# Mask products exchanged between VectorE and GpSimd, copies of keys and queries moved, and global outputs normalized for two quads at a time in the steady batches of an attention and feed-forward kernel

## The chip, the cores and the metric

The kernel runs on one core of a Trainium2 chip. The metric is the device time of one execution in microseconds (us). Before the change the median of three runs is 285.36 us (285.32 to 285.50).

## The reference

Eight batches (B = 8) of eight heads (H = 8) with 512 local and 32 global positions each, and a head dimension of 64. A local query sees all 32 global keys and the local keys at most 32 positions away; a global query sees everything. The outputs of all heads of one position form a row of 512, and each of the 4352 rows goes through a feed-forward layer with a sigmoid-approximated GELU.

```python
k_all = np.concatenate([k_g, k_l], axis=2)
v_all = np.concatenate([v_g, v_l], axis=2)
out_g = np.matmul(sm(scale * np.matmul(q_g, k_all.transpose(0, 1, 3, 2))), v_all)
mask = np.abs(pos[:, None] - pos[None, :]) <= 32
s_ll = np.where(mask, scale * np.matmul(q_l, k_l.transpose(0, 1, 3, 2)), -1000000000.0)
s_lg = scale * np.matmul(q_l, k_g.transpose(0, 1, 3, 2))
out_l = np.matmul(sm(np.concatenate([s_lg, s_ll], axis=-1)), v_all)
x = np.concatenate([out_g, out_l], axis=2).transpose(0, 2, 1, 3).reshape(4352, 512)
h = x @ w_in                                   # 4352 x 2048
out = (h * (1.0 / (1.0 + np.exp(-1.702 * h)))) @ w_out
```

## The kernel before

**Tiling.** The four heads of one half of a batch are a quad: 16 quads, two to a batch, called `a` (first) and `c` (second). A quad's keys and queries lie four heads by 32 partitions, as pairs of bf16 numbers in f32 words, so that one 32x32 transpose of f32 words (`Tk`, L512, and `Tq`, L316) puts the head dimension on partitions. Because of the window, the local scores of a quad are computed in two rounds of parts (`S(0)`, `S(1)`, L560): each is a set of 32-row matmuls into four PSUM banks, then an exponential on ScalarE (`X`, L571, two instructions), then a product in place with a 0/1 mask of bf16 (`M`, L576).

For these parts a quad needs some copies: `kcopy` (L504) and `qcopy` (L507) put keys and queries that lie apart side by side, and `ext` (L538 to L545, four parts) puts the global queries and keys beside the local ones. `transpose_g` (L244) transposes global queries and keys.

**Outputs of attention.** `U(0)` sums the masked exponentials with a matrix of ones, `U(1)` and `U(2)` multiply them with the two halves of the values (L586, 24 matmuls each), and `Gm` (L597, 20 matmuls) gives the numerators and denominators of the global queries in one bank `og`. `UG` is all four. `R` (L462 to L466) transposes the sums, takes reciprocals and transposes back; `XL(0)` and `XL(1)` (L471) write the normalized local outputs `xL`. `G` (L476 to L479) takes the reciprocal of the denominator in `og`, multiplies, and transposes into `xG`, which the feed-forward layer reads as a ninth block at the very end.

**Feed-forward.** `h_step` (L617) makes 128 of the 2048 hidden features for one batch's 512 local rows, `h_act` (L622) applies the GELU. One pair of features blocks is made in seven products instead of eight, as a Strassen scheme (`HPair`, L699), from sums of `xL` that `x_sums` (L673, L674) makes on VectorE; its additions are `z`, `zm`, `sub`, `add` (L707 to L716), its GELUs `inner` and `outer`. The second matrix is done for all of a batch in the same scheme, in two halves of rows: `Pair` (products L800; `m3` and `evict` on ScalarE, L113; `z`, `zm`, `sub`, `add` on VectorE, L812 to L825; `store` by SP's queue). Its left sums `g_sums` (L770, L773) are on VectorE.

**Order.** The order is written out by hand (no scheduler): each engine runs its instructions in the order of the program, and waits at semaphores. From i = 3 on a batch alternates between two stages. `h_some(i)` is the first matrix of batch i (its first TensorE line is `hp L617 x8`); between its steps come the transposes and copies for quad `c` of batch i+1 and quad `a2` of batch i+2. `phase_o(i)`, called for i = 2 to 6, is the second matrix of batch i (`p0`, `p1`) interleaved with the rest of the attention of batch b = i+1: quad `a` was scored before, `c` is scored in it, and so is quad `a2` of batch i+2. Its `loads_after(i + 1)` issues on GpSimd's queue the nine transfers of values (L98, L100) and the two of queries and keys (L81, L82) of later batches, with a cast from f32 to bf16.

**PSUM.** The scores and the pair of `HPair` share four banks. The other four (pool `psP`, tag `p`) are handed out in turn. In `phase_o` the order is: `a`'s three `ov` and `og`, then px and py of `p0`, `c`'s three `ov` and `og`, then px and py of `p1`, then the `hp` of the next stage. So px of `p0` takes the bank of `a`'s U(0) once `R` has transposed it, `c.U(2)` takes the bank of px of `p0` once `evict` has read it, and the third `hp` of `h_some` to use this pool (feature block 4) takes px of `p1`.

Of the kernel before, what the change touches and what calls it, by code (L numbers as in the profile page):

```python
# [12 lines left out]
F32 = mybir.dt.float32  # L13
BF16 = mybir.dt.bfloat16
# [6 lines left out]
def kernel(  # L21
# [12 lines left out]
    nc = tc.nc  # L34

    B, H, Sl, D = q_l.shape
# [23 lines left out]
    att = ctx.enter_context(tc.tile_pool(name="att", bufs=2))  # L60
# [14 lines left out]
    def load(b, us=(0, 1), kq=True):  # L75
        if b not in loaded:
            loaded[b] = (ld.tile([128, 2, 16 * D], BF16, name="rk"),
                         ld.tile([128, 2, 16 * D], BF16, name="rq"))
        if kq:
            s = slice(us[0], us[-1] + 1)  # L80
            nc.gpsimd.dma_start(out=loaded[b][1][:, s], in_=qf[b][:, s])  # L81
            nc.gpsimd.dma_start(out=loaded[b][0][:, s], in_=kf[b][:, s])  # L82
# [8 lines left out]
    def load_v(b, hs=slice(0, 8)):  # L91
        if b == 2:
            nc.gpsimd.memset(v_view(b, 5)[:, :, :, :, D:], 1.0)
        vt = v_view(b, 5).rearrange("p u j c d -> p (u j) c d")
        vs, vg = (x[b].rearrange("h s d -> s h d") for x in (v_l, v_g))
        for c in range(5):
            n = 128 if c == 2 else 96
            nc.gpsimd.dma_start(out=vt[0:n, hs, c, :D], in_=vs[FIRST[c] : FIRST[c] + n, hs])  # L98
            if c != 2 and b != 1:
                nc.gpsimd.dma_start(out=vt[96:128, :, c, :D], in_=vg)  # L100
# [11 lines left out]
    def on_act(out_, in_):  # L112
        nc.scalar.activation(out_, in_, AF.Copy)  # L113
# [11 lines left out]
    def load_g(lo, hi, names="kq"):  # L125
        for name, dst, src in (("k", rkg, kgf), ("q", rqg, qgf)):
            if name in names:
                nc.gpsimd.dma_start(out=dst[:, lo:hi, :], in_=src[:, lo:hi, :])
# [111 lines left out]
    def transpose_g(lo, hi, names="qk"):  # L240
        for name, dst, s in (("q", qgT, rqg), ("k", kgT, rkg)):
            if name not in names:
                continue
            nc.vector.transpose(dst[:, lo:hi, :32], s[:, lo:hi].bitcast(F32))  # L244
# [31 lines left out]
    xG_by_row = xG.rearrange("p k (a s f) -> p k a s f", a=2, f=4)  # L276
# [7 lines left out]
    def spair():  # L284
        return [psS.tile([128, 2, 512], F32, name="s4", tag="s%d" % i) for i in range(2)]

    def bank(pair, j):
        return pair[j // 2][:, j % 2, :]
# [211 lines left out]
    class Wide(Quad):  # L500
# [100 lines left out]
        def UG(self):  # L601
            for unit in range(3):
                self.U(unit)
            self.Gm()

    gTs, ops = {}, {}
    HT = TB // 2
    HM = d_model // 2
# [23 lines left out]
    def gelu_table():  # L632
        gelu(spot[:, 0:1], spot[:, 1:2])

    def exp_table():
        nc.scalar.activation(spot[:, 0:1], spot[:, 1:2], AF.Exp)
# [27 lines left out]
    def x_sums(i):  # L664
        t = xL[i]
        x11, x12, x21, x22 = (t[:, 2 * k : 2 * k + 2, h * HT : h * HT + HT] for k in range(2) for h in range(2))
        r1 = att.tile([128, 16, 32], F32, name="sT", bufs=1).rearrange("p a b -> p (a b)").bitcast(BF16)
        r2 = att.tile([128, 512], F32, name="rs", bufs=1).bitcast(BF16)
        xs["d"] = [r.rearrange("p (k t) -> p k t", k=2) for r in (
            r1[:, : 2 * HT], r1[:, 2 * HT :], moe.tile([128, 2 * HT], BF16, name="xs"))]  # L670
        xs["s"] = r2.rearrange("p (k t) -> p k t", k=NKC)
        for o, x, y, op in zip(xs["d"], (x11, x12, x21), (x22, x22, x11), (ALU.add, ALU.subtract, ALU.subtract)):
            nc.vector.tensor_tensor(o, x, y, op)  # L673
        nc.vector.tensor_tensor(xs["s"], t[:, :, :HT], t[:, :, HT:], ALU.add)  # L674
        xs["r"] = (x11, x22)
# [173 lines left out]
    a, c = Quad(0), Quad(1)  # L849
# [93 lines left out]
    a, c = nq[1]  # L943
# [71 lines left out]
    a, c = nq[2]  # L1015
# [22 lines left out]
    def loads_after(i):  # L1038
        if i + 2 < B:
            load_v(i + 2)  # L1040
        if i == 1:
            load_g(8, NQ)
        if i + 3 < B:
            load(i + 3)

    def quads_of(n):
        if n < B and n not in nq:
            nq[n] = (Wide(2 * n), Wide(2 * n + 1))
        return nq.get(n, (None, None))
# [44 lines left out]
    def phase_o(i):  # L1094
        b = i + 1
        a, c = nq[b]
        a2, c2 = quads_of(b + 1)
        p0, p1 = Pair(i, 0), Pair(i, 1)
        exp_table()
        a.UG()  # L1100
        c.S(0)
        a.R()
        g_sums(i, 7, 8, (0,))
        a.XL(0)
        g_sums(i, 7, 8, (1, 2))
        a.XL(1)
        g_sums(i, 7, 8, (3,))
        p0.mm(3, 4, 1)
        c.X(0)
        p0.m3()  # L1110
        p0.z()
        a.G()
        c.M(0)
        c.S(1)
        c.X(1)
        p0.mm(6)
        p0.zm()
        c.M(1)
        p0.mm(5, 2)
        p0.sub()  # L1120
        p0.evict()
        p0.mm(7)
        p0.add()
        p0.store()
        if a2:
            c.UG()
            c.R()
            a2.S(0)
            a2.X(0)
            a2.M(0, nc.gpsimd)  # L1130
            loads_after(i + 1)
        else:
            pt = spair()
            c.U(0, bank(pt, 0))
            c.U(1, bank(pt, 2))
            c.U(2, bank(pt, 3))
            c.Gm(bank(pt, 1))
            c.R()
        c.XL(0)
        if a2:  # L1140
            c.XL(1)
            c.G()
        p1.mm(3, 4)
        p1.m3()
        p1.z()
        if not a2:
            c.XL(1)
            c.G()
        p1.mm(1, 6)
        p1.zm()  # L1150
        x_sums(i + 1)
        if a2:
            a2.S(1)
            a2.X(1)
        p1.mm(5, 2)
        p1.sub()
        p1.evict()
        gelu_table()
        p1.mm(7)
        p1.add()  # L1160
        if a2:
            a2.M(1)
        p1.store()

    def h_some(i):
        c = nq[i + 1][1] if i + 1 < B else None
        a2 = quads_of(i + 2)[0] if i + 2 < B else None
        pool = nc.gpsimd.tensor_copy
        gTs[i] = moe.tile([128, FC, TB], BF16, name="gT")
        hps = [pbank("hp"), pbank("hp")]  # L1170
        for fc in range(2):
            h_mm(i, fc, hps[fc], range(NKC))
        p = HPair(i, 1)
        p.mm(3, 4)
        p.m3()
        for fc in range(2):
            h_act(i, fc, hps[fc])
        if c:
            c.Tk(False)
            c.kcopy(pool)  # L1180
        p.z()
        p.mm(1, 6)
        p.zm()
        if c:
            c.Tq(False)
            c.qcopy(pool)
            c.ext((3,), pool)
        if a2:
            a2.Tk(False)
            a2.kcopy(pool)  # L1190
        h_step(i, 4)
        if c:
            c.ext((0,), on_act)
        h_step(i, 5)
        p.mm(5, 2)
        p.sub()
        p.inner()
        p.mm(7)
        p.add()
        h_step(i, 6)  # L1200
        p.outer()
        if a2:
            a2.Tq(False)
            transpose_g(2 * i + 4, 2 * i + 6)
            a2.qcopy(pool)
            a2.ext(copy=pool)
        if c:
            g_sums(i, 0, 2)
        h_step(i, 7)
        if c:  # L1210
            c.ext((1,), on_act)
            g_sums(i, 2, 4)
            for fc in range(8, 12):
                h_step(i, fc)
                if fc == 9:
                    c.ext((2,), on_act)
            g_sums(i, 4, 6)
            h_step(i, 12)
            h_step(i, 13)
            g_sums(i, 6, 7)  # L1220
            h_step(i, 14)
            h_step(i, 15)
            return
        p = HPair(i, 4)
        p.mm(3, 4)
        p.m3()
        g_sums(i, 0, 2, (0, 1))
        p.z()
        p.mm(1, 6)
        p.zm()  # L1230
        g_sums(i, 0, 2, (2,))
        h_step(i, 10)
        h_step(i, 11)
        p.mm(5, 2)
        p.sub()
        p.inner()
        p.mm(7)
        p.add()
        g_sums(i, 0, 2, (3,))
        h_step(i, 12)  # L1240
        p.outer()
        for k in range(3):
            for lo in (2, 4):
                g_sums(i, lo, lo + 2, (k,))
        h_step(i, 13)
        h_step(i, 14)
        h_step(i, 15)
        g_sums(i, 6, 8, (0, 1, 2))
        g_sums(i, 2, 4, (3,))
        g_sums(i, 4, 6, (3,))  # L1250
        g_sums(i, 6, 8, (3,))

    for i in range(1, B):
        if i > 2:
            h_some(i)
        elif i > 1:
            for fc in range(FC):
# [3 lines left out]
                if i + 1 < B:  # L1261
                    c = nq[i + 1][1]
# [6 lines left out]
                    if fc == 9 and i + 2 < B:  # L1269
                        a2 = quads_of(i + 2)[0]  # L1270
# [19 lines left out]
    for st in range(FC):  # L1290
        h_step(B, st)
        if st < len(todo):
            tt, k = todo[st]
            if k == 3:
                p = Pair(B - 1, tt, pair_banks(tt))
# [19 lines left out]
    p = Pair(B, 0, (x0, x1, y0, y1))  # L1315
# [53 lines left out]
```

## Time and profile before

| what | value |
|---|---|
| median of three runs | 285.36 us |
| the profiled execution | 285.70 us |
| its span, first to last instruction | 284.0 us |
| granted TensorE clock | 1.00 |
| busy: TensorE, VectorE, ScalarE, GpSimd | 277.0, 228.9, 182.1, 107.1 us |
| phase_o(3), 131.0 to 148.6 us: VectorE, ScalarE, GpSimd busy (of 17.65) | 16.4, 10.8, 4.7 us |
| h_some(4), 148.7 to 163.7 us: VectorE, ScalarE, GpSimd busy (of 15.00) | 14.7, 12.1, 9.4 us |

The profile names PE (TensorE), DVE (VectorE), ACT (ScalarE), POOL (GpSimd) and SP (SyncE, which issues the stores). A line of the chain of waits or of a timeline gives start and duration in us, engine, operation, what it writes and reads, and how many of them; in brackets stands the idle time of the engine before it and what ended it. A `kT<-kT` on POOL is a kcopy, a `qc<-q` a qcopy, an `e<-e,mask` an M, an `sT<-xL` the first two x_sums, `gs<-gT` are g_sums.

### The profile page before, as it was taken

How to read it: one execution, taken by the hardware profiler on the slowest of the kernel's cores; microseconds unless marked ns; L12 is line 12 of the kernel's file. 1: busy time of each engine (PE TensorE's matmuls, PEld its weight loads, DVE VectorE, ACT ScalarE, POOL GpSimd, SP SyncE). 2: the span in 40 equal slices, each digit the busy share in tenths (PEclk: the TensorE clock that was granted, in tenths of full speed). 3: DMA queues.
4: the chain of work that ended last, by engine and by line, in shares of the span. 5: the costliest groups of instructions: out<-in, count | busy, mean ns of one | idle time of the engine just before them, and what ended most of it. 6: DMA issues, size and time to landing. Idle time of an engine off the chain costs nothing.

```text
span 284.0 us, 9001 instructions
## 1 busy us (share of the span) xinstructions
PE 277.0 (98%) x3763; PEld 182.3 (64%) x3763; DVE 228.9 (81%) x518; ACT 182.1 (64%) x299; POOL 107.1 (38%) x172
## 2 busy tenths in 40 slices
PE   7899999999999999999999999999999999999994
PEld 6454445544554488746885588647875589558884
DVE  7584458986689899999989998999988898586452
ACT  4858757577778784688457873788459761873331
POOL 8993550765946001990079302960041000000001
PEclk9999999999999999999999999999999999999999
DMA  7999995899999801795039802980022003200223
GB/s 208 159 195 210 203 162 77 148 217 144 170 165 183 151 2 48 78 177 91 14 69 163 150 5 68 84 97 3 21 58 74 2 3 76 74 3 0 58 54 112
DMA packets 59352, 28.24 MB, mean 99 GB/s; under 512 B 47472, under 2 KB 49776, under 8 KB 59312
## 3 DMA queue, kind: packets, MB, share of 16 engines
q0 software_dynamic: 51760, 17.83, 56.2%
q1 hardware_dynamic: 7120, 9.18, 11.7%
q8 instruction: 29, 0.48, 0.7%
q10 hardware_dynamic: 432, 0.66, 0.7%
q14 instruction: 11, 0.09, 0.1%
HBM read 36.31 MB, written 8.91 MB: 159 GB/s over the span
## 4 chain that ended last, share of the span: by engine, by line
PE 86%; DVE 7%; DMA 2%; issue 1%; POOL 1%; ACT 1%; DVEq 0%; POOLq 0%; ACTq 0%
PE hp L617 31%; PE px L800 12%; PE op L731 10%; PE py L800 9%; PE x L800 6%; PE s L560 5%; PE ov L586 5%; PE s L699 3%; PE s L617 3%; DMA rq<-in_q_l_dram 2%; DVE gs L773 2%; DVE gs L770 1%; DVE xL L471 1%; DVE kT L512 1%; PE og L597 1%
## 5 line engine op out<-in xcount | busy, mean ns | idle before, releaser
L617 PE MATMUL hp<-xL,w_in_sb 128*128 128x512 bf16 x432 | 97.0, 379 | 0.2 <-DVE xL L471 0.2
L617 PEld LDWEIGHTS <-w_in_sb 128*128 128x128 bf16 x528 | 51.4, 98 | 51.8 <-issue 0.4
L622 ACT ACTIVATE gT<-hp 128x512 bf16<-128x512 f32 x108 | 62.7, 600 | 17.1 <-PE hp L617 16.6
L571 ACT ACTIVATE e<-s 128x1016 bf16<-128x1016 f32 (+1 forms) x56 | 53.3, 1003 | 25.7 <-PE s L560 25.7
L800 PEld LDWEIGHTS <-gs 128*128 128x128 bf16 x480 | 46.2, 98 | 6.6
L576 POOL TENSOR_TENSOR e<-e,mask 128x1760 bf16<-128x1760 bf16 x4 | 13.3, 3320 | 70.0 <-ACT e L571 70.0
L98 POOL DMA_DIRECT2D v<-in_v_l_dram x40 | 31.1, 780 | 13.6 <-PE og L597 3.8
L773 DVE TENSOR_TENSOR gs<-gT 128x512 bf16<-128x512 bf16 (+1 forms) x87 | 31.6, 398 | 3.3 <-ACT gT L622 3.3
L800 PE MATMUL py<-wsum,gs 128*128 128x256 bf16 x240 | 30.3, 273 | 0.0
L731 PE MATMUL op<-w_out_sb,gT 128*128 128x512 bf16 x128 | 29.5, 380 | 0.0
L576 DVE TENSOR_TENSOR e<-e,mask 128x1712 bf16<-128x1712 bf16 (+1 forms) x24 | 25.2, 1049 | 3.5 <-ACT e L571 3.5
L512 DVE STREAM_TRANSPOSE kT<-rk 128x512 f32<-128x512 f32 x14 | 14.5, 1037 | 12.6 <-DMA rk<-in_k_l_dram 12.6
L833 POOL DMA_DIRECT2D out_dram<-ob x2 | 1.2, 596 | 60.5 <-ACT ob L113 60.3
L731 PEld LDWEIGHTS <-gT 128*128 128x128 bf16 x128 | 11.8, 98 | 14.0
L800 PEld LDWEIGHTS <-gT 128*128 128x128 bf16 x192 | 18.0, 98 | 3.0
L800 PE MATMUL px<-w_out_sb,gT 128*128 128x256 bf16 x160 | 19.2, 273 | 0.1
L800 PE MATMUL px<-w_out_sb,gs 128*128 128x256 bf16 x160 | 19.1, 273 | 0.0
L471 DVE TENSOR_TENSOR xL<-ov,rs 128x512 bf16<-128x512 f32 x27 | 17.9, 686 | 1.0 <-PE ov L438 0.3
L113 ACT ACTIVATE ob<-px 128x512 f32<-128x512 f32 x10 | 6.0, 599 | 19.3 <-DVE zz L822 19.3
L770 DVE TENSOR_TENSOR gs<-gT 128x1024 bf16<-128x1024 bf16 (+1 forms) x29 | 17.2, 598 | 0.0
L560 PEld LDWEIGHTS <-kT 32*128 32x128 bf16 x672 | 12.5, 93 | 6.8 <-issue 5.7
L100 POOL DMA_DIRECT2D v<-in_v_g_dram x24 | 14.0, 585 | 2.2 <-DMA rq<-in_q_l_dram 1.7
(176 smaller groups left out, 429.3 us busy)
## 6 DMA issues: line engine op xcount, KB each, us to landing
out_dram<-ob SPq DMA_DIRECT2D x128, 64.0 KB, 2.7
rq<-in_q_l_dram POOLq DMA_DIRECT2D x5, 512.0 KB, 8.2
rk<-in_k_l_dram POOLq DMA_DIRECT2D x5, 512.0 KB, 10.0
v<-in_v_l_dram POOLq DMA_DIRECT2D x24, 96.0 KB, 4.8
w_in_sb<-in_moe_w_in_dram POOLq DMA_DIRECT2D x8, 256.0 KB, 6.9
w_out_sb<-in_moe_w_out_dram POOLq DMA_DIRECT2D x4, 512.0 KB, 10.1
rk<-in_k_l_dram POOLq DMA_DIRECT2D x5, 256.0 KB, 7.8
rq<-in_q_l_dram POOLq DMA_DIRECT2D x5, 256.0 KB, 7.2
```

The lines of the kernel that those rows point to most:

```text
L98: nc.gpsimd.dma_start(out=vt[0:n, hs, c, :D], in_=vs[FIRST[c] : FIRST[c] + n, hs])
L471: nc.vector.tensor_mul(self.x[:, 2 * self.u + h, :], self.st[1 + h], self.st["rs"])
L512: nc.vector.transpose(flat[:, 0:Sl].rearrange("p (r t) -> p t r", t=16), loaded[self.b][0][:, self.u].bitcast(F32))
L560: nc.tensor.matmul(bank(self.ps, j)[:, at : at + n], lhsT=self.k[p, KEYS[c] : KEYS[c] + 128, e], rhs=qs[p, :, :, e], start=(e == 0), stop= ...
L571: nc.scalar.activation(self.E[rnd][:, 2 * i : 2 * i + 2, :n], self.ps[i][:, :, :n], AF.Exp, scale=scale)
L576: eng.tensor_mul(e, e, mask[:, rnd : rnd + 1, :n].to_broadcast([128, 4, n]))
L617: nc.tensor.matmul(hp[:, : width(i)], lhsT=w_in_c[:, fc // 4, kc, fc % 4 // 2, :, fc % 2], rhs=(xL[i] if i < B else xG)[:, kc, :], start=( ...
L622: nc.scalar.activation(out_, in_, AF.Gelu_apprx_sigmoid)
L731: nc.tensor.matmul(op, lhsT=gTs[i][:, fc, tci * 128 : tci * 128 + 128], rhs=w_out_sb[:, fc, :], start=(first and fc == 4 * f4), stop=(fc = ...
L770: nc.vector.tensor_tensor(sums[i][2][:, g, :n], t[:, g, 0, :n], t[:, g, 1, :n], ALU.add)
L773: nc.vector.tensor_tensor(sums[i][k][:, g, : n // 2], x[:, g], y[:, g], op)
L800: nc.tensor.matmul(out_, lhsT=lv[:, g, tt * 128 : tt * 128 + 128], rhs=rv[:, g, :], start=(g == 0 and k in ((1, 3, 4, 6) if self.apart els ...
```

## The change

In `phase_o`, for all of its calls:
- `a.G()` and `c.G()` are gone. `keep_og` copies each quad's `og` from PSUM to an SBUF tile `ogs` on ScalarE (66 columns), and `GG` normalizes both quads at once on VectorE: one reciprocal, one product, two transposes.
- `a2.M(0)` moves from GpSimd to VectorE, and from behind `a2.X(0)` to behind `p1.z()`; `a2.M(1)` moves from VectorE to GpSimd.
- `loads_after` moves out of `phase_o` into the following `h_some`, behind the copies of `c` on GpSimd.

In `h_some(i)`, i from 3: the transposes of `c` and `a2` come earlier in VectorE's order, ahead of the additions of `HPair`. The kcopy, qcopy and ext of `a2`, which GpSimd did there, move to ScalarE in the following `phase_o` (i = 3 to 5): kcopy and qcopy ahead of the exponential `c.X(1)`, ext behind it.

TensorE's instructions and their order are the same. (`i > 2` and `a2` together are i = 3, 4, 5.)

```diff
+    def keep_og(q, ogs):
+        on_act(ogs[:, q.u], q.st["og"][:, : D + 2])
+
+    def GG(b, ogs):
+        rg = att.tile([128, 2, 1], F32, name="rgg")
+        nc.vector.reciprocal(rg, ogs[:, :, D : D + 1])
+        xg = att.tile([128, 2, D], BF16, name="xgg")
+        nc.vector.tensor_mul(xg, ogs[:, :, :D], rg.to_broadcast([128, 2, D]))
+        for u in range(2):
+            nc.vector.transpose(xG_by_row[:, 2 * u : 2 * u + 2, b // 4, :, b % 4],
+                                xg[:, u].rearrange("p (d h) -> p h d", h=2))
...
@@ def phase_o(i):
+        ogs = att.tile([128, 2, D + 2], F32, name="ogs", bufs=1)
+        late = a2 and i > 2
...
         p0.m3()
         p0.z()
-        a.G()
+        keep_og(a, ogs)
+        if late:
+            a2.kcopy(on_act)
+            a2.qcopy(on_act)
         c.M(0)
         c.S(1)
         c.X(1)
         p0.mm(6)
         p0.zm()
         c.M(1)
+        if late:
+            a2.ext(copy=on_act)
         p0.mm(5, 2)
...
         if a2:
             c.UG()
             c.R()
+            keep_og(c, ogs)
             a2.S(0)
             a2.X(0)
-            a2.M(0, nc.gpsimd)
-            loads_after(i + 1)
...
         c.XL(0)
         if a2:
             c.XL(1)
-            c.G()
+            GG(b, ogs)
         p1.mm(3, 4)
         p1.m3()
         p1.z()
-        if not a2:
+        if a2:
+            a2.M(0)
+        else:
             c.XL(1)
-            c.G()
+            GG(b, ogs)
...
         p1.add()
         if a2:
-            a2.M(1)
+            a2.M(1, nc.gpsimd)
         p1.store()
@@ def h_some(i):
         if c:
             c.Tk(False)
             c.kcopy(pool)
+            c.Tq(False)
+            c.qcopy(pool)
+            c.ext((3,), pool)
+            loads_after(i)
+        if a2:
+            a2.Tk(False)
         p.z()
         p.mm(1, 6)
         p.zm()
-        if c:
-            c.Tq(False)
-            c.qcopy(pool)
-            c.ext((3,), pool)
         if a2:
-            a2.Tk(False)
-            a2.kcopy(pool)
+            a2.Tq(False)
+            transpose_g(2 * i + 4, 2 * i + 6)
         h_step(i, 4)
...
         p.outer()
-        if a2:
-            a2.Tq(False)
-            transpose_g(2 * i + 4, 2 * i + 6)
-            a2.qcopy(pool)
-            a2.ext(copy=pool)
```

More of the change, by code (lines that the diff above doesn't have):

```diff
@@ L1138, in phase_o @@
             c.R()
+            keep_og(c, ogs)
         c.XL(0)
```

## The prediction

> **What bounds the kernel now.** I read the page first, then the chain of waits, then the timelines of VectorE, GpSimd and ScalarE around one steady batch. The page's first and fourth parts:
>
> ```profile
> PE 277.0 (98%) x3763; PEld 182.3 (64%) x3763; DVE 228.9 (81%) x518; ACT 182.1 (64%) x299; POOL 107.1 (38%) x172
> ...
> PE 86%; DVE 7%; DMA 2%; issue 1%; POOL 1%; ACT 1%; DVEq 0%; POOLq 0%; ACTq 0%
> ```
>
> TensorE is occupied for 277.0 of 284.0 us, at a granted clock of 1.00 in every stage. A shift of work between the other engines can pay only where TensorE waits for them. The chain of waits in order of time shows where that is (start, duration, what):
>
> ```profile
> 117.44 1.73 PE hp L617 x8
> ...
> 147.52 0.41 DVE sT L673
> ...
> 156.71 1.98 DVE gs L773 x2
> ...
> 163.78 0.64 DVE sT L462
> 164.46 1.91 PE px L800 x16
> ...
> 180.35 1.73 PE hp L617 x8
> ...
> 211.66 1.73 PE hp L617 x8
> ```
>
> The `hp L617 x8` lines shown open h_some(3), h_some(5) and h_some(6). From 180.35 to 211.66 one batch takes 31.31 us. From 117.44 to 180.35 two take 62.91, which is 0.29 more than twice 31.31. In between the chain leaves TensorE and runs through VectorE from 145.5 to 164.4: the first product px of phase_o(4) waits for the transpose sT that frees its bank. So the steady batches hold some 0.3 us of TensorE time that another engine owns; elsewhere in them the chain is matmul after matmul. The rest of TensorE's idle time lies in the first 21 us and the last 28, which the change does not touch.
>
> Why VectorE is late there, from the timelines of VectorE and GpSimd (start, duration; brackets: idle before):
>
> ```profile
> 143.99 3.32 POOL L576 TENSOR_TENSOR e<-e,mask 128x1760 bf16<-128x1760 bf16 x1 [16.21 <-ACT e L571]
> ...
> 145.86 2.07 DVE L673 TENSOR_TENSOR sT<-xL 128x512 bf16<-128x512 bf16 x2
> 147.85 0.41 DVE L673 TENSOR_TENSOR xs<-xL 128x512 bf16<-128x512 bf16 x1
> ...
> 155.57 0.52 POOL L507 COPY qc<-q 128x384 bf16<-128x384 bf16 x1
> ...
> 156.71 1.98 DVE L773 TENSOR_TENSOR gs<-gT 128x512 bf16<-128x512 bf16 x2
> ...
> 159.21 1.08 DVE L773 TENSOR_TENSOR gs<-gT 128x512 bf16<-128x512 bf16 x3
> ```
>
> Two x_sums of one shape as the third (0.41, next start 0.34 later) take 2.07: the chain above has the second start at 147.52, just after GpSimd's mask product ends (147.31). The first two g_sums take 1.98 where three later take 1.08: GpSimd's copies run until 158.4. The f32 transposes and the additions with one operand in PSUM keep their times beside GpSimd (L316 0.70 at 152.88 and at 155.75, L812 0.41 and 0.40). So what loses time to GpSimd's reads is a product or sum with both inputs in SBUF: 1.3 us in each x_sums, 1.2 in these g_sums.
>
> **The change, part by part** (times of batch i=3 and h_some(4), the rows above).
>
> TensorE's instructions and their order stay; only waits can move.
>
> *Masks.* a2.M(0) goes to VectorE (L576, 1.06), a2.M(1) to GpSimd (3.32 x 1712/1760 = 3.23). On VectorE that is 1.06 in for 1.04 out. M(0) now stands between z and zm: XL ends at 143.75, then the new GG, z, M(0) to about 146.0, zm to 146.35, x_sums to 147.95 without GpSimd beside them, against 148.87 now. Sub then waits for nothing but TensorE's product 2 (147.74). M(1) starts when the second exponential ends, 146.09 + 1.89 = 147.98 plus the 0.08 that M(0) shows, so at 148.06; the last x_sum starts at about 147.3, 0.75 before. Behind M(1) on GpSimd's queue stand c.kcopy, c.qcopy, c.ext(3), then the loads: copies 151.3 to 152.6, needed by c.S(0) at 163.7. M(1) itself is needed by a.UG at 162.3. Eleven us of cover; without it, its 3.2 us would be on the path.
>
> *Loads.* Nine for v (5 x 0.78 + 4 x 0.585) and two for q and k (2 x 0.66), 7.6 us of GpSimd's issue, move behind those copies and start at 152.6 instead of 147.3. They end near 160.2 and land about 10 us later (page, part 6); the next key transpose that needs them is at 182.7. Their wait for the query transpose (0.31) is gone. Price nothing.
>
> *Global outputs.* Out on VectorE: two G of 0.16 + 0.28 + 0.32 = 0.76 each. In: one GG with 0.16, a product of 128x128 (between 0.28 for 128x64 and 0.41 for 128x256; I take 0.33), two transposes of 0.32: 1.13. VectorE gains 0.4 a batch, but 0.7 of it early, while the second half is some 0.3 to 0.4 longer.
>
> *Key and query copies.* a2.kcopy, qcopy and ext leave GpSimd for ScalarE in phase_o(3) to (5). No such copy is in the trace on ScalarE, but its rows give a line: 128x144 from SBUF 0.325, 128x512 0.629, so 0.206 + 0.83 ns per element: kcopy (192) 0.37, qcopy (384) 0.52, ext 0.33, 0.33, 0.28 and 0.42. The 128x66 keep_og from PSUM, by 0.386 for 256 and 0.599 for 512, 0.23. Neighbours overlap by about 0.10 (0.37 at 151.57, next at 151.84). ScalarE's idle time, from its timeline:
>
> ```profile
> 134.90 0.39 ACT L113 ACTIVATE zz<-px 128x256 f32<-128x256 f32 x1
> ...
> 136.35 1.89 ACT L571 ACTIVATE e<-s 128x992 bf16<-128x992 f32 x2 [1.06 <-PE s L560]
> ...
> 139.95 0.60 ACT L113 ACTIVATE ob<-px 128x512 f32<-128x512 f32 x1 [1.72 <-DVE zz L822]
> ...
> 141.98 1.93 ACT L571 ACTIVATE e<-s 128x1016 bf16<-128x1016 f32 x2 [1.43 <-PE s L560]
> ```
>
> Ahead of X(1): keep_og, kcopy, qcopy, 1.12 end to end, 0.82 with overlap, into 1.06 (1.14 and 1.03 in the other two batches). Behind it: ext, 1.36 at most, into 1.72. Then keep_og of c, 0.23 into 1.43. So nothing waits, or X(1) comes up to 0.09 late. That matters, because behind X(1) stand M(1) of c, sub, and the eviction that frees the bank of c.U(2): it ends at 140.55, and U(2) starts at about 140.6 (units start 139.85, 140.22, so 0.37 apart). There is 0.05 us to spare. By the upper price the loss is 0.09 - 0.05 a batch, 0.1 in three; by the lower, none. I take none, as the overlap is seen wherever two such copies follow each other.
>
> *h_some.* Without M(1) on VectorE and with x_sums earlier, the four big transposes stand ahead of sub and add: Tk 149.4, Tq, Tk to 152.0, z (was 152.04) 0.2 later, add some 0.3 to 0.9 earlier. The first g_sums still wait for ScalarE's outer gelu (156.04 at present, up to 1 earlier), and run with no copy beside them: 1.2 less. VectorE reaches sT at about 162.5 instead of 163.78, and TensorE's own product of U is last again.
>
> *The sum.* TensorE gets back 0.29 in phase_o(4), nothing elsewhere: 2, 3 and 5 show no wait to remove. The profiled execution took 285.70, its span 284.0; 285.4 after. The median 285.36 lies 0.34 below that execution; 285.36 - 0.29 = 285.1.
>
> [...] The trace shows the x_sums held for the whole of GpSimd's product. [...]
>
> **The rivals.**
> *ScalarE becomes late (slower).* If each of kcopy and qcopy costs what the longest SBUF row costs, 0.63, the three take 1.49, X(1) is 0.43 late, the eviction too, and c.U(2) waits 0.38 in three batches: 1.15 less the gain, 286.2. It decides once the copies pass 1.11 us. Against it: the rows' straight line. For it: 0.05 us of slack at the bank.
> *GpSimd's M(1) catches the last x_sum (slower).* Then that sum waits until 151.3 and ends at 151.9; product 6 of the Strassen pair, due at 150.99, waits 0.9, and the bank of p1.x comes some 1.1 late for fc 4. Two us in four batches: about 293. It decides if VectorE's chain is over 0.75 us later than my sum. For it: GG and M(0) are both put into that chain. Against: 0.75 is over twice what is unknown in GG.
> *The gain is given back (no change).* If the big transposes do wait for GpSimd's M(1) (until 151.3), z comes at 154, outer gelu at 157.7, and the six us of g_sums end at 163.6 as now: 285.4, in each batch alike. L316 beside L507 speaks against it.
> *More bubbles than I see (faster).* c.UG takes 1.24 against 1.20 for a.UG, px after S 1.85 against 1.75; if several went, 0.6 in all: 284.75.
>
> **How the numbers follow.** About 0.2% (0.57 us) is what a measurement of this kernel can tell from no change. Gain of 0.3, 285.1: 0.60. Given back, 285.4: 0.15. ScalarE late, 286.2: 0.10. Lock, 293: 0.05. Other new waits of under 1 us in several batches: 0.04. More bubbles: 0.06. Faster 0.06, same 0.75, slower 0.19. The range, 284.8 to 286.3, takes in the first three and leaves out some 0.15; the likeliest case's own is 284.9 to 285.4.
>
> **What would show it.** Right: the x_sums in one run of about 1.7 us, ended before GpSimd's 3.2 us product starts; sT in phase_o(4) with TensorE as its releaser; hp L617 openings 31.31 apart throughout; ScalarE still idle before X(1) for `PE s L560`. Wrong: X(1) with no idle before it, L586 of c split by a wait, an x_sum of 3 us, or hp openings further apart than 31.4.

## The result, and the profile after

| kernel | median | range | runs | ratio to before, 95% interval |
|---|---|---|---|---|
| before | 285.50 us | 285.30 to 286.26 | 9 | |
| changed | 286.76 us | 286.00 to 287.99 | 9 | 1.0042 (1.0024 to 1.0060) |

The changed kernel is slower by 0.4%, and its executions lie further apart (2.0 us from lowest to highest, against 1.0). The profiled execution has a span of 285.5 us. The page's first and fourth parts of the changed kernel:

```profile
PE 275.2 (96%) x3740; PEld 181.8 (64%) x3763; DVE 220.3 (77%) x508; ACT 190.0 (67%) x327; POOL 99.1 (35%) x154
...
PE 92%; DMA 2%; DVE 2%; issue 1%; POOL 1%; ACT 1%; DVEq 0%; POOLq 0%
```

VectorE has lost 8.6 us of busy time, GpSimd 8.0, ScalarE has won 7.9, and VectorE's share of the chain has gone from 7% to 2%. That is what the change set out to do, and yet the span is 1.5 us longer. The chain of waits of the changed kernel shows where:

```profile
117.27 1.67 PE hp L629 x7
...
130.84 1.20 PE ov L586 x61
...
135.50 0.41 PE s L560 x14
135.91 1.49 issue
137.41 0.42 PE s L560 x8
...
150.31 1.67 PE hp L629 x7
...
181.61 1.67 PE hp L629 x7
...
212.91 1.67 PE hp L629 x7
```

(Lines from L605 on have moved: `hp` is L629 now, L812 the products of Pair, L711 those of HPair, L685 and L686 the x_sums, L785 and L782 the g_sums.) The h_some stages open 33.04, 31.30 and 31.30 us apart. The 0.29 us that phase_o(4) lost before is won back, to the hundredth. But the batch from 117.27 to 150.31 is 1.74 too long, and 1.49 of it is one wait in the middle of c.S(1) of phase_o(3). (Most of the rest is the row of matmuls that the wait cuts in two: 0.41 and 0.42 in the chain, where the kernel before has 0.56.) Its label "issue" means that nothing in the profile released it. TensorE and ScalarE around it, from the timeline of the changed kernel:

```profile
134.95 0.24 ACT L113 ACTIVATE ogs<-og 128x66 f32<-128x66 f32 x1
...
135.05 0.38 ACT L113 ACTIVATE kT<-kT 128x192 f32<-128x192 f32 x1
...
135.31 0.54 ACT L113 ACTIVATE qc<-q 128x384 bf16<-128x384 bf16 x1
...
135.54 0.37 PE L560 MATMUL s<-q,kT 32*128 32x228 bf16 x6
...
137.41 0.42 PE L560 MATMUL s<-q,kT 32*128 32x228 bf16 x10 [1.49 <-issue]
...
137.81 1.89 ACT L571 ACTIVATE e<-s 128x992 bf16<-128x992 f32 x2 [1.96 <-PE s L560]
```

Six of sixteen equal matmuls ran, then none for 1.49 us, then the other ten. Nothing they need shows as late: GpSimd's copies of `c` ended at 120.9, the exponential that reads the scores before had ended at 134.8, and the loads of weights stood still as well (1.76 us, also "issue"). ScalarE had done its copies and waited 1.96 us for TensorE.

So I turned to the instructions themselves. The page's list of DMA queues has one that carries instructions in the largest packets; I call one of its packets a fetch (queue, packets, MB, share of 16 engines' span):

```profile
q8 instruction: 29, 0.48, 0.7%
```

Twenty-nine packets of 16 KB by the packet records. The page of the kernel before counts 3763 matmuls and 3763 loads of weights for TensorE, and 518 instructions for VectorE, the most of any other engine. So I take these packets for TensorE's, and estimate from the counts some 260 instructions in each (7526 / 29); no view names their engine. By the trace's packet records the first one in phase_o(3) started 1.52 us after the stage opened in the kernel before (132.50, opening 130.98), and 4.39 us after it in the changed kernel (135.23, opening 130.84); there it took 0.97 us, and TensorE went on 1.2 us after its end. What the DMA engines did meanwhile, in three stretches. (In us: busy time and count of PE, PEld, DVE, ACT and POOL, then granted clock, DMA share, GB/s. The DMA share adds up the times of the packets that start in the stretch; they can overlap, so it can exceed 1, as 2.22 in experiment 10.) The kernel before first:

```profile
131.00:133.00 2.00, 2.00 (x118) 1.83 (x118) 1.97 (x7) 1.88 (x3) 0.00 (x0) 1.00 0.22 42
133.00:135.00 2.00, 2.00 (x19) 1.75 (x20) 1.97 (x6) 2.00 (x4) 0.00 (x0) 1.00 0.00 0
135.00:137.00 2.00, 2.00 (x38) 1.54 (x37) 1.93 (x8) 0.94 (x3) 0.00 (x0) 1.00 0.03 8
```

and the changed kernel:

```profile
131.00:133.00 2.00, 2.00 (x117) 1.81 (x108) 1.56 (x3) 1.97 (x4) 0.00 (x0) 1.00 1.09 193
133.00:135.00 2.00, 2.00 (x20) 1.80 (x19) 2.00 (x7) 2.00 (x4) 0.00 (x0) 1.00 0.99 186
135.00:137.00 2.00, 0.91 (x19) 0.41 (x17) 1.57 (x4) 0.85 (x4) 0.00 (x0) 1.00 0.12 24
```

Before, the loads have all but ended when phase_o(3) opens: 33 of the 512 packets of the query and key transfer are left. Now this transfer, issued by GpSimd at 127.1 and 127.8 (before: 122.6 and 123.2), has 396 of them left, and keeps the DMA engines busy until about 135.2. This gives a theory, F: the moved loads delay TensorE's instruction fetch. The rival, E: one of the moved instructions of ScalarE, VectorE or GpSimd holds TensorE up in the executions that were not profiled.

### The profile page after: what moved, and what is told of

Same layout as the page of the kernel before. It is cut to its first block, busy times and chain, and to the rows that moved or that the text cites. A ratio compares the mean times of both kernels' runs of the same rounds, so it can differ in the third digit from the quotient of the medians.

```text
span 285.5 us, 8970 instructions
## 1 busy us (share of the span) xinstructions
PE 275.2 (96%) x3740; PEld 181.8 (64%) x3763; DVE 220.3 (77%) x508; ACT 190.0 (67%) x327; POOL 99.1 (35%) x154
## 4 chain that ended last, share of the span: by engine, by line
PE 92%; DMA 2%; DVE 2%; issue 1%; POOL 1%; ACT 1%; DVEq 0%; POOLq 0%
PE hp L629 34%; PE px L812 13%; PE op L743 10%; PE py L812 9%; PE x L812 6%; PE s L560 6%; PE ov L586 5%; PE s L711 3%; PE s L629 2%; DMA rq<-in_q_l_dram 2%; DVE xL L471 1%; PE og L597 1%; ACT e L385 0%; DVE sT L462 0%; PE s L357 0%
## 5 line engine op out<-in xcount | busy, mean ns | idle before, releaser
L629 PE MATMUL hp<-xL,w_in_sb 128*128 128x512 bf16 x417 | 95.6, 379 | 0.9 <-DVE xL L471 0.2
L629 PEld LDWEIGHTS <-w_in_sb 128*128 128x128 bf16 x528 | 51.3, 98 | 51.9 <-issue 0.4
L812 PEld LDWEIGHTS <-gs 128*128 128x128 bf16 x480 | 46.2, 98 | 6.4
L576 POOL TENSOR_TENSOR e<-e,mask 128x1712 bf16<-128x1712 bf16 x4 | 12.9, 3236 | 85.6 <-ACT e L571 85.6
L785 DVE TENSOR_TENSOR gs<-gT 128x512 bf16<-128x512 bf16 (+1 forms) x87 | 29.7, 371 | 7.1 <-ACT gT L634 7.0
L812 PE MATMUL py<-wsum,gs 128*128 128x256 bf16 x240 | 30.3, 273 | 0.0
L743 PE MATMUL op<-w_out_sb,gT 128*128 128x512 bf16 x122 | 28.8, 380 | 0.5 <-issue 0.3
L576 DVE TENSOR_TENSOR e<-e,mask 128x1760 bf16<-128x1760 bf16 (+1 forms) x24 | 25.3, 1053 | 5.2 <-ACT e L571 5.2
L812 PEld LDWEIGHTS <-gT 128*128 128x128 bf16 x192 | 18.0, 98 | 2.9
L812 PE MATMUL px<-w_out_sb,gT 128*128 128x256 bf16 x160 | 19.2, 273 | 0.0
L812 PE MATMUL px<-w_out_sb,gs 128*128 128x256 bf16 x160 | 19.1, 273 | 0.0
L782 DVE TENSOR_TENSOR gs<-gT 128x1024 bf16<-128x1024 bf16 (+1 forms) x29 | 17.1, 593 | 0.0
L560 PE MATMUL s<-q,kT 32*128 32x160 bf16 (+1 forms) x448 | 15.0, 246 | 1.5 <-issue 1.5
```

Source lines behind the costliest of these rows:

```text
L560: nc.tensor.matmul(bank(self.ps, j)[:, at : at + n], lhsT=self.k[p, KEYS[c] : KEYS[c] + 128, e], rhs=qs[p, :, :, e], start=(e == 0), stop= ...
L576: eng.tensor_mul(e, e, mask[:, rnd : rnd + 1, :n].to_broadcast([128, 4, n]))
L629: nc.tensor.matmul(hp[:, : width(i)], lhsT=w_in_c[:, fc // 4, kc, fc % 4 // 2, :, fc % 2], rhs=(xL[i] if i < B else xG)[:, kc, :], start=( ...
L743: nc.tensor.matmul(op, lhsT=gTs[i][:, fc, tci * 128 : tci * 128 + 128], rhs=w_out_sb[:, fc, :], start=(first and fc == 4 * f4), stop=(fc = ...
L782: nc.vector.tensor_tensor(sums[i][2][:, g, :n], t[:, g, 0, :n], t[:, g, 1, :n], ALU.add)
L785: nc.vector.tensor_tensor(sums[i][k][:, g, : n // 2], x[:, g], y[:, g], op)
```

## The experiments

In each, "before" is the kernel before on the same chip. Offsets of the fetch are counted from the opening of phase_o(3), in us, and "issue wait" is a wait with that label.

**1. The loads back in phase_o.**

```diff
             c.ext((3,), pool)
-            loads_after(i)
...
             a2.M(0)
+            loads_after(i + 1)
```

> The changed kernel with one part undone: loads_after(i + 1) stands in phase_o again (behind p1.z), not in h_some. Theory F (fetch): the changed kernel loses time because its loads now move data while TensorE's next 16 KB of instructions are due; in its profile TensorE stands still for 1.49 us in the middle of c.S(1) of phase_o(3) with no releaser, and the fetch of its instruction queue only starts when the loads have ended. With the loads back ahead of h_some the stall goes and the 0.3 us of phase_o(4) stays won: 285.0 to 285.3, no TensorE idle time put down to issue in the steady batches. Rival E (engines): the copies on ScalarE, the mask product on GpSimd or GG hold TensorE up in most executions: then putting the loads back changes nothing, 286.2 to 287.

Measured: 285.50 us against 285.56, ratio 0.9995 (0.9986 to 1.0004); no issue wait in the steady batches, the fetch at 1.54. The loss goes with the loads; everything else of the change stayed in. The median is 0.2 above what I expected.

**2. The loads alone moved, in the kernel before.**

```diff
             a2.M(0, nc.gpsimd)
-            loads_after(i + 1)
...
             a2.kcopy(pool)
+        if c:
+            loads_after(i)
```

> The kernel before with the loads alone moved: loads_after goes from phase_o into the following h_some, behind a2.kcopy on GpSimd, some 2.5 us later than in the changed kernel. Theory F: TensorE's instruction fetch meets the loads as in the changed kernel or worse: 286.2 to 288, with a stall of 1 to 3 us put down to issue in phase_o(3) or phase_o(4). Rival E: the loads are needed a batch later, nothing moves: 285.2 to 285.6.

Measured: 287.88 us (286.57 to 290.60) against 285.56, ratio 1.0082 (1.0053 to 1.0111). TensorE's waits in its profile:

```profile
PE s L560 <- issue: 1.9, 1, 1.9
```

The same place, 1.90 instead of 1.49; the loads stand some 2.5 us later than in the changed kernel, and the fetch started at 4.70. None of the other parts of the change is in this kernel, so E falls: the moved loads are enough for the loss, and by 1 they are needed for it.

**3. No loads.** The loads that h_some issues are left out.

> The changed kernel without the loads that h_some issues: batches 6 and 7 use the queries and keys of batches 4 and 5, and batches 5 to 7 the values already in their tile. All other instructions stay. Theory F: nothing is left to delay the fetch; 285.0 to 285.2, steady batches 31.3 us apart throughout. Rival E: 286.2 to 287, as the changed kernel.

Measured: 285.25 us against 285.56, ratio 0.9985 (0.9977 to 0.9994); fetch at 1.35, openings 31.3 apart. This is the change without its cost.

**4. The loads in two parts.**

```diff
             c.ext((3,), pool)
-            loads_after(i)
+            if i + 3 < B:
+                load(i + 3)          # queries and keys
...
             a2.M(0)
+            if i + 3 < B:
+                load_v(i + 3)        # values
```

> The changed kernel with the loads in two parts: the nine of the values in phase_o behind p1.z (GpSimd idles there from 131 to 149 us and the tile is free after c.UG), the two of queries and keys in h_some behind GpSimd's copies of c. Theory F: GpSimd issues the last load some 6 us earlier than in the changed kernel, the transfers end before the next phase_o, and the mask product on GpSimd waits for no load: 285.0 to 285.3. If the values' transfers meet a fetch inside phase_o instead, a stall of 1 us shows in its second half: 286. Rival E: 286.2 to 287.

Measured: 285.25 us (285.12 to 285.81) against 285.56, ratio 0.9990 (0.9981 to 0.9998), fetch at 1.44. The values are issued while GpSimd is idle, the queries and keys are issued 6.4 us sooner than in the changed kernel (at 120.6 and 121.4), and they are over when the next phase_o opens (DMA share 0.03 from 131 to 133, where the changed kernel has 1.09). This version beats the changed kernel and, by 0.1% and at the edge of the interval, the kernel before. Its h_some stages open as they should, in the chain of waits:

```profile
117.08 1.67 PE hp L629 x7
...
148.37 1.67 PE hp L629 x7
...
179.67 1.67 PE hp L629 x7
...
210.97 1.67 PE hp L629 x7
```

**5 and 6. Which of the loads.** In 5 only those of h_some(3) go back into phase_o(2); in 6 only those of h_some(3) stay late.

```diff
-            loads_after(i)
+            if i > 3:                # experiment 6: if i == 3
+                loads_after(i)
...
             a2.M(0)
+            if i == 2:               # experiment 6: if i > 2
+                loads_after(i + 1)
```

> The changed kernel with only the loads that h_some(3) issues put back into phase_o(2); those of h_some(4) and h_some(5) stay late. Theory F (loads delay TensorE's instruction fetch): the profiles of the changed kernel and of the kernel with the loads alone moved show one stall each, in c.S(1) of phase_o(3), so these eleven transfers should carry nearly the whole loss: 285.2 to 285.6. If phase_o(4) stalls too in executions that were not profiled, 285.8 to 286.3. If the loss is not in the place of the loads but in something that all batches share: 286.2 or more.

> The counterpart of the kernel with only the first loads back: here the loads of h_some(3) stay late, and those of h_some(4) and h_some(5) go back into phase_o. If the stall in c.S(1) of phase_o(3) is what the changed kernel loses, it loses as much here: 286.3 to 287.2 with 1 to 2 us of issue in c.S(1) of phase_o(3). If the later loads carry a good part (the kernel with the first loads back kept some 0.45 us of loss against the split loads), 285.6 to 286.2.

Measured: 5: 285.86 us against 285.31, ratio 1.0006 (0.9991 to 1.0022), no issue wait in its profile. 6: 286.82 us against 285.86, ratio 1.0035 (1.0016 to 1.0054), with a wait of 0.66 in c.S(1) and the fetch at 3.48. So the eleven transfers ahead of phase_o(3) carry most of the loss. In 5 the next late fetch (3.85 us into phase_o(4)) did not stop TensorE in the profiled execution; whether it does in others, which would explain why 5 is not as fast as 3, stays open.

The profiled executions together give a scale for phase_o(3): fetch at 1.35, 1.44, 1.52 and 1.54: no wait; at 3.48: 0.66; at 4.39: 1.49; at 4.70: 1.90. The offset exceeds the wait by 2.82, 2.90 and 2.80; from these three I estimate that beyond some 2.8 us every us of delay is a us lost there. The figure does not hold for phase_o(4): there the fetch started 3.6 us after the opening in the changed kernel and 5.1 us after it in experiment 2, and neither execution waited for it.

**7 and 8. The edge of the block moved.** A block is what one fetch brings. 32 small matmuls more at the start, in the changed kernel (7) and in the kernel with split loads (8).

```diff
     fill(8, a.bk[1][3])
+    for _ in range(32):
+        nc.tensor.matmul(a.bk[1][3][:, :8], lhsT=warm0, rhs=warm0[:, :8], start=False, stop=False, ...)
```

> The changed kernel with 32 small matmuls more at the start (8 columns, adding zeros, while TensorE waits for data), so that every later TensorE instruction sits 64 places further on in its stream and the edge of each 16 KB block falls 32 matmuls earlier in the program. Nothing else differs. Theory F: the fetch still ends when the loads let it, 6.6 us into phase_o(3), but TensorE runs out of instructions 32 matmuls earlier, in p0's px at about 3.0 us into the stage instead of 5.1: the stall grows from 1.5 to about 3.5 us and moves from S (L560) to the products (L812): 288 to 289.5. Rival (the stall is bound to that place in the program, a PSUM bank or a semaphore of c.S(1)): it stays in S(1), 1.5 us, 286.2 to 287.2 as the changed kernel.

> The same 32 small matmuls in the kernel with split loads (values in phase_o, queries and keys in h_some). It shows what the extra matmuls and the moved block edges cost where no load is late. Theory F: 285.2 to 285.8, with at most 0.3 us of stall where the block is now due sooner. Rival (the extra matmuls themselves cost the time): as much more than 285.25 as e6 is more than the changed kernel.

Measured: 7: 287.12 us, ratio 1.0060 (1.0041 to 1.0080); 8: 286.95 us, ratio 1.0052 (1.0035 to 1.0069), both against 285.31. My figures missed in both. In 7 the wait in phase_o(3) did not grow, it was gone: h_some(3) and h_some(4) open 31.30 apart. And both kernels got a new one elsewhere, in the first products of the feed-forward near 19 us. The line stands alike in TensorE's waits of 7 and of 8; behind it the place, from TensorE's timeline of 7:

```profile
PE s L629 <- issue: 1.0, 1, 1.0
...
19.43 1.24 PE L629 MATMUL s<-xL,w_in_sb 128*128 128x512 bf16 x5 [1.01 <-issue]
```

A fetch ended 1.4 us before TensorE went on (17.06 to 18.03 in 7); in the changed kernel one ran from 17.38 to 18.33. I had the fetch of phase_o(3) come 0.5 us sooner in the stage. But 32 matmuls sooner in the program is, it seems, already the end of h_some, where a matmul takes 0.22 us: the fetch ran 3.6 us ahead of phase_o(3), among the 128-byte packets of the values and before those of queries and keys. What I had as the rival, that the wait is bound to c.S(1), its bank or its semaphores, is refuted: with the same instructions there, the wait disappears, and one comes up behind another fetch. With this placement the late loads cost next to nothing (1.0060 against 1.0052).

**9 and 10. Which transfer holds the fetch.** 9 leaves out the queries and keys and keeps the values late; 10 issues the queries and keys first and then the values, at the same place in h_some.

```diff
             c.ext((3,), pool)
-            loads_after(i)
+            if i + 3 < B:
+                load(i + 3)          # left out in experiment 9
+            if i + 2 < B:
+                load_v(i + 2)
```

> The changed kernel without the loads of queries and keys in h_some (batches 6 and 7 use those of batches 4 and 5); the nine loads of values stay where they are, as late as in the changed kernel. In the changed kernel's profile the instruction fetch of 135.2 us starts just as the 2 KB packets of the query and key transfer run out; in the shifted kernel a fetch ran at once between the 128-byte packets of the values. Theory Q (only the query and key transfers hold the fetch): 285.0 to 285.3, no stall. Theory V (any load traffic does, by its amount): the values end some 3 us into phase_o at most, a shorter stall: 285.6 to 286.3.

> The changed kernel with the two parts of its loads in the other order, at the same place in h_some: queries and keys first, then the nine of values. The same bytes, ended at the same time; only what is under way when TensorE's fetch of phase_o(3) is due differs, values instead of queries and keys. Theory Q: 285.0 to 285.4, with no stall in c.S(1). Theory V: as the changed kernel, 286.2 to 287.

Measured: 9: 285.62 us, ratio 1.0000 (0.9989 to 1.0012), fetch at 1.14. 10: 285.57 us, ratio 0.9997 (0.9988 to 1.0006), fetch at 1.87; both against 285.57, without an issue wait in the steady batches. 10 moves the same bytes from the same place and loses nothing. What its DMA engines did after phase_o(3) opened:

```profile
131.00:133.00 2.00, 2.00 (x117) 1.80 (x116) 1.43 (x3) 1.96 (x3) 0.00 (x0) 1.00 2.22 147
```

With the values' 128-byte packets under way (share 2.22, 147 GB/s) the fetch is 0.5 late; with the 2 KB packets of queries and keys (1.09, 193 GB/s) it was 3 late. But the loads did not end at the same time, as I had expected: by the packet records the last packet of 10 starts at 133.08, that of the changed kernel at 136.19, and in both the fetch starts as the packets run out (132.84 and 135.23). In 9 the values have ended at 129.2, before phase_o(3) opens, so they had nothing to hold. The two experiments show that without the query and key transfer in that place there is no loss, and that the other order avoids it; that the values would hold the fetch for less time if they ran as late is not shown. Two things speak for it. The fetch of 7 started with packets of the values both before and behind it. And by an estimate from the packet times (0.17 us for 2 KB, 0.03 for 128 bytes) every delay, 0.5 us here and 2 to 3.3 in experiments 2 and 6 and the changed kernel, is the time of some 12 to 19 packets one after the other: a fetch that waits behind so many packets would fit, but no run tests it. Both medians lie 0.1% above those of 3 and 4, at the edge of what the intervals tell apart.

**11. The masks alone.** The kernel before with the mask exchange and split loads.

```diff
-            a2.M(0, nc.gpsimd)
-            loads_after(i + 1)
...
         p1.z()
+        if a2:
+            a2.M(0)
+            if i + 3 < B:
+                load_v(i + 3)
...
-            a2.M(1)
+            a2.M(1, nc.gpsimd)
```

> The kernel before with the mask exchange alone (a2.M(0) on VectorE behind p1.z, a2.M(1) on GpSimd) and the loads split as in e4; G, the copies on GpSimd and the transposes' order as before. The x_sums no longer lie beside a GpSimd product, which frees 1.3 us of VectorE a batch, more than the 0.29 us by which phase_o(4) was late: 285.2 to 285.3, sT of phase_o(4) released by TensorE. If the copies on GpSimd beside the first g_sums (1.2 us) were what made phase_o(4) late, it stays at 285.5 and sT still follows g_sums without idle time.

Measured: 285.13 us against 285.31, ratio 0.9993 (0.9976 to 1.0009): too small for the times, but the profile is plain. Openings 31.29, 31.31 and 31.30 apart, and sT of phase_o(4) waits for TensorE. From VectorE's timeline:

```profile
161.78 0.28 DVE L773 TENSOR_TENSOR gs<-gT 128x256 bf16<-128x256 bf16 x1
162.43 0.72 DVE L462 STREAM_TRANSPOSE sT<-ov 128x512 f32<-128x512 f32 x1 [0.37 <-PE ov L586]
```

The exchange, with the loads split, recovers the 0.29 us. The x_sums take 0.74 for two instead of 2.07, and the first two g_sums 1.01 instead of 1.98; which of the two would have been enough is not separated.

**12. The masks put back.** The kernel with split loads, with a2.M(0) on GpSimd behind a2.X(0) and a2.M(1) on VectorE, as before, and the loads of values behind a2.M(0).

> The kernel with split loads, with the mask products where they were before (a2.M(0) on GpSimd, a2.M(1) on VectorE): copies on ScalarE, GG and the earlier transposes stay. The x_sums lie beside GpSimd's product again and take some 2.07 us for two, but no copy lies beside the first g_sums (1.2 us freed). Expected: that alone covers the 0.29 us by which phase_o(4) was late, openings of the h_some stages 31.3 apart, 285.2 to 285.4. If the masks are the part that matters: phase_o(4) late by 0.3 again, 285.4 to 285.6.

Measured: 289.03 us, ratio 1.0120 (1.0107 to 1.0133). Expected by neither side. TensorE's waits name a new one:

```profile
PE s L711 <- DVE ob L719: 2.5, 3, 0.9
```

The changed order in h_some puts two Tk and a Tq ahead of z. With M(1) and the x_sums, which take 2.0 for two again, also ahead of them, z (L719) comes too late for TensorE's products 5 and 2, which add into the tile that z reads: 0.8 to 0.9 us in each of three batches. The early transposes live off the room that the mask exchange makes, so the parts cannot be priced one by one and added up.

## Why the prediction was wrong

Wrong by the term "Loads ... Price nothing". I checked who needs the data (a batch later, as it proved) and which queue the issue occupies, but not what else moves by DMA at that time. The prediction's own figures had the loads landing near 170, some 8 us into phase_o(4). The move costs 1.49 us of waiting in the profiled execution of the changed kernel (0.66 and 1.90 in experiments 6 and 2), in one place, and about 0.4% of the median. The sum also began from "only waits can move" and listed waits for engines; a fetch of TensorE's own instructions was in no term and in none of the rivals, so the range of 284.8 to 286.3 ended below 286.76.

The other steps held, one by one:
- *Masks.* All four x_sums run in one piece of 1.68 us (1.7 foreseen), and the last starts 1.0 us ahead of GpSimd's product. In VectorE's and GpSimd's timelines of the changed kernel:

```profile
147.58 0.74 DVE L685 TENSOR_TENSOR sT<-xL 128x512 bf16<-128x512 bf16 x2
148.24 0.42 DVE L685 TENSOR_TENSOR xs<-xL 128x512 bf16<-128x512 bf16 x1
148.58 0.68 DVE L686 TENSOR_TENSOR rs<-xL 128x1024 bf16<-128x1024 bf16 x1
...
149.59 3.24 POOL L576 TENSOR_TENSOR e<-e,mask 128x1712 bf16<-128x1712 bf16 x1 [21.05 <-ACT e L571]
```

- *Copies.* keep_og 0.24, kcopy 0.38, qcopy 0.54 where 0.23, 0.37 and 0.52 were worked out. In phase_o(4) and phase_o(5), where no stall hides it, ScalarE still waited 0.25 for TensorE ahead of X(1), where the kernel before has 1.14 and 1.03: the copies fitted in, by the lower price. The rival "ScalarE becomes late" did not occur.
- *Global outputs.* GG took 0.15, 0.29 and 0.47 for both transposes: 0.9 instead of 1.13, because the two transposes overlap (0.47 together, where the kernel before has 0.32 for one).
- *h_some.* Counted from the opening of h_some(4), the additions came 0.4 to 0.9 earlier (z too, which I had 0.2 later), and the first g_sums ran without a copy beside them, 0.76 for two instead of 1.98. The rivals "M(1) catches the last x_sum" and "the gain is given back" did not occur either: f32 transposes ran at 1.04, 0.66 and 1.00 beside or right behind GpSimd's product.
- *The sum.* TensorE got back 0.29 in phase_o(4): openings 31.30. Experiments 3 and 4 stand 0.1% to 0.15% below the kernel before, as foreseen for the whole; experiment 1 stands 0.05% below it, which its interval does not tell from no change. And sT of phase_o(4) waits for TensorE again, in VectorE's timeline of the changed kernel:

```profile
164.40 0.72 DVE L462 STREAM_TRANSPOSE sT<-ov 128x512 f32<-128x512 f32 x1 [0.56 <-PE ov L586]
```

The term "Lock, 293" of the forecast stands for the rival "M(1) catches the last x_sum". No run shows a lock as such. What the runs show is two x_sums in 2.07 us beside GpSimd's product (the kernel before), in 0.74 ahead of it (the changed kernel and experiment 11), and in 2.0 with the masks put back (experiment 12).

What stays open: why that transfer holds the fetch so long (in experiment 2 the fetch ran while it was still under way, 3.3 us late, so it is not simply the end of the transfer that counts); whether any transfer that runs as late would do the same; and whether the later fetch, in phase_o(4), costs time in executions that were not profiled (no profile shows it).

## What to carry to other kernels

Before a transfer is moved, look at what else moves by DMA at the new time. Here a dense stretch of small matmuls (118 in 2 us, with as many loads of weights) uses up, by the estimate of 260 instructions to a block, a block in some 2.2 us, and with the query and key transfer under way the next fetch started 2 to 3.3 us later. A wait put down to "issue" in the middle of a row of equal matmuls was the sign here. 32 matmuls more ahead of it showed that it was not bound to that place in the program, but put a stall of 1.0 us elsewhere (7 and 8), so it is a test and no cure. In this kernel it was enough to put the query and key transfer where the instruction stream is thin (the 0.22 us matmuls of h_some), so early that it has ended when the dense stage opens, as the split does (experiment 4, ratio 0.9990). With the other order (10) the last load ended 2.1 us into the stage, which was early enough here.

## What the runs showed of the hardware

In phase_o(3) a fetch that started up to 1.87 us after the opening (experiment 10) stopped nothing; one that started 3.48, 4.39 and 4.70 us after it stopped TensorE for 0.66, 1.49 and 1.90 us (experiment 6, the changed kernel, experiment 2). That the loss begins at some 2.8 us is my estimate from these three. In phase_o(4) one that started 5.1 us after the opening stopped nothing (experiment 2). The fetch itself takes 0.9 to 1.6 us (29 in the trace of each of the two kernels); its start in phase_o(3) varies by more, from 1.14 (experiment 9) to 4.70 (experiment 2). With a transfer in 2 KB packets under way that start came 3 us later (the changed kernel), with one in 128-byte packets, which ended 2.1 us into the stage, 0.5 us later (experiment 10).
